# A Fourier mixing kernel with an ELU layer: one channel's transform, its loads and a batch's later transforms set to later steps

## The chip, the cores and the metric

The kernel runs on one core of a Trainium2 chip. Its time is the device time of one execution in microseconds (us); the figure used is the median over several executions. One further execution is recorded by the hardware profiler, and all rows of a profile in this text come from such an execution.

## The reference

```python
# x: (8, 3008, 256), w_in: (256, 2048), w_out: (2048, 256), all float32
X = np.fft.fft(x, axis=1)
X = np.fft.fft(X, axis=2)
attn = X.real.astype(np.float32)              # (8, 3008, 256)
h = attn.reshape(24064, 256) @ w_in
g = np.where(h > 0.0, h, np.exp(np.minimum(h, 0.0)) - 1.0)
out = (g @ w_out).astype(np.float32)
```

Each of the 8 batches is transformed along its 3008 rows and its 256 channels; only the real part is kept. Every row then goes through two matrix products with an ELU between them.

## The kernel before

**What is computed where.** The real part of the double transform is even in a joint mirroring of row and channel, so the kernel keeps two rings in SBUF, `Rr` (real) and `Ir` (imaginary), with the folded channels in their 128 partitions and half of the rows (1504 per batch, `HALF`) as columns. The channel transform is folded into the first weights (`Wc`, `Ws`). The channels are counted by 0 to 127 in the partitions; channel 128 is left over and is handled for all 8 batches together, in its own small transform. Its result is put into a third ring, `Rb`, which holds one row repeated in all partitions, and into partition 127 of `Ir`.

**Steps.** The columns of all batches are cut in 47 tiles of 256, and each tile in 8 steps (two blocks of 128 of the 2048 hidden units each): 376 steps in all. In a step TensorE forms `P` = Wc x Rr (`mm_P`), VectorE adds the part of channel 128 (`even_part`, tile `E`, line 764), TensorE adds `Q` = Ws x Ir onto the same PSUM bank `H`, and VectorE forms the mirrored half (`h_minus`, line 774). ScalarE makes the exponentials of both halves (line 394), VectorE the ELU (`g_plus`, `g_minus`, line 790, tile `G`). GpSimd forms four sums of blocks of `G` (`sum_1` to `sum_4`, line 391), and TensorE uses blocks and sums in seven products with `w2` and `WT` (`mm_X1`, `mm_X2`, PSUM banks `pA` to `pD`, line 382): a product scheme that needs seven multiplications for eight. Step n's second products are issued two steps later. After a tile's 8 steps the four banks are combined on ScalarE and VectorE (`comb_copy` with tile `p`, `comb_1`, `comb_2`, `comb_22`, `comb_3` with tiles `u` and `v`, line 388), transposed (`turn_u`, `turn_v`, lines 935 and 956, tile `ot`) and stored by SyncE (`store`, line 988, many small DMAs).

**Transforms.** A batch is loaded in four tiles `xl0` to `xl3` (`load_x`: `xl3` and `xl0` by SyncE, lines 168 and 169; `xl2` and `xl1` by indirect DMAs of GpSimd, line 157). GpSimd folds them in 16 operations of two pieces each (`fold_x`, line 476, tiles `e` and `o`); the results EO0, EO2, EO1 and EO3 feed four transforms (`at_dft`), real and imaginary part for even and odd rows. Each transform is done in two halves of three matrix products with the constant tiles `MC`, one at the end of a step and one at the end of the step two later. ScalarE copies the first half to a buffer `bs` (two buffers), and VectorE adds and subtracts both into the ring (`plus`, `minus`).

**Channel 128.** `load_ext` loads it in 16 pieces: four rows (j = 0 to 3) of 768 samples for 8 batches, four pieces each, sample by sample (line 613). When a row is there, it is stored to DRAM (`xe_dr`, line 631). `get_ext` loads all back in another layout (`xs`, line 637); `fold_ext` folds on GpSimd (`xe`); `dft_ext` is 12 products of 8 columns each, 24 instructions of TensorE; `ext_side` copies three parts to `bs` buffers on ScalarE; `ext_rows` combines them to `rx`, once on VectorE and once on GpSimd, and stores to DRAM (`r128`, lines 705 and 708); `spread_ext` loads a batch's part into `Rb` and `Ir` (lines 715 and 719).

**The order.** All is written as a list of events with due times in units of a step, `T = PERIOD`, and the list is sorted and issued. The due time sets only the place in the order of each engine; each engine then runs its instructions in that order as soon as what they wait for is there.

```python
    def at(t, fn):
        events.append((t, len(events), fn))
...
    for _, _, fn in sorted(events, key=lambda e: e[:2]):
        fn()
```

Computing instructions, the single-channel loads and `load_x`'s indirect loads of batch 1 are held in that order (`pin`); the other DMAs, among them `get_ext`, the output stores, the loads of `xl3` and `xl0` and `spread_ext`, are placed on SyncE's queue by the framework, which may put them elsewhere between the pinned ones. SyncE's queue issues in order and uses eight semaphores in turn, so that it waits for an earlier DMA's end before it issues the eighth after it.

Of the kernel before, what the change touches and what calls it, by code (L numbers as in the profile page):

```python
# [90 lines left out]
def kernel(  # L91
# [58 lines left out]
    def load_x(b):  # L150
        L = [
            spool.tile([128, 6 * ND], FP, tag=f"xl{j}", bufs=1, name=f"xl{j}")
            for j in range(4)
        ]
        for j in (2, 1):
            c = 1 if j == 2 else 2 if b == NB - 1 else 0
            load = nc.gpsimd.indirect_dma_start(
                out=L[j],
                out_offset=None,
                in_=xflat,  # L160
                in_offset=bass.IndirectOffsetOnAxis(
                    ap=ix[:, c : c + 1].bitcast(U32), axis=0
                ),
                element_offset=b * SEQ * ND,
            )
            if b == 1:
                pin(load)
        nc.sync.dma_start(out=L[3], in_=xrows(b, HALF, 6, 128))
        nc.sync.dma_start(out=L[0], in_=xrows(b, 0, 6, 128))
        if b == NB - 1:  # L170
            nc.gpsimd.dma_start(
                out=L[1][0:1, 0 : 5 * ND], in_=xrows(b, SEQ - 5, 1, 1, 5)
            )
        return L
# [218 lines left out]
    def act(o, i, func=AF.Copy, **kw):  # L393
        pin(nc.scalar.activation(out=o, in_=i, func=func, **kw))  # L394
# [211 lines left out]
    def load_ext(j, s0, s1):  # L606
        if j == 0 and s0 == 0:
            state["x1"] = spool.tile([128, HALF + 1], FP, tag="rx", bufs=1, name="x1")
        t = state["x1"][j * NB : (j + 1) * NB]

        def copy(s0, s1, row, step):
            pin(
                nc.sync.dma_start(
                    out=t[:, s0:s1],
                    in_=bass.AP(
                        tensor=xt,
                        offset=x.offset + row * ND + 128,
                        ap=[[SEQ * ND, NB], [step * ND, s1 - s0], [1, 1]],
                    ),
                )  # L620
            )

        with nc.allow_non_contiguous_dma(reason="one channel"):
            if j == 1 and s0 == 0:
                copy(0, 1, 0, 1)
                copy(1, s1, SEQ - 1, -1)
            else:
                step = -1 if j in (1, 2) else 1
                copy(s0, s1, (0, SEQ, HALF, HALF)[j] + step * s0, step)
        if s1 == 768:  # L630
            nc.sync.dma_start(out=xe_dr[j], in_=t[:, 0:768])
# [50 lines left out]
    def ext_side(g, rows=NB):  # L682
        n = NO if g > 1 else NE
        t = spool.tile([128, NE], FP, tag="bs", bufs=2, name="bs")
        act(t[0:rows, 0:n], state["ext"][32 * g : 32 * g + rows, 0:n])
        state["side", g] = t[0:rows, 0:n]

    def ext_rows(kodd, tt, rows=NB):
        n = NO if kodd else NE
        if not kodd or rows < NB:  # L690
            rx = spool.tile([128, HALF + 1], FP, tag="rx", bufs=1, name="rx")
            state["rx"] = rx[0:rows]
        if not kodd:
            a = state["ext"][0:NB, 0:n]
        else:
            a = state["side", 2]
        rx, b = state["rx"], state["side", 2 * kodd + 1]
        o, base = 1 - kodd, kodd * RUN
        m = n - 2 * o
        tt(rx[:, base : base + n], a, b, ALU.add)  # L700
        top = base + RUN - 1
        tt(rx[:, top : top - m : -1], a[:, o : o + m], b[:, o : o + m], ALU.subtract)
        if not kodd:
            tt(rx[:, HALF:], a[:, 0:1], b[:, 0:1], ALU.subtract)
            nc.sync.dma_start(
                out=r4_dr.rearrange("o b -> b o"), in_=rx[:, HALF : HALF + 1]
            )
        nc.sync.dma_start(
            out=r128_dr[0:rows, base : base + RUN], in_=rx[:, base : base + RUN]
        )  # L710

    def spread_ext(b, kodd):
        for sl, a, z in ring_cut(b * HALF + kodd * RUN, RUN, False):
            a, z = a + kodd * RUN, z + kodd * RUN
            nc.sync.dma_start(
                out=Rb[:, sl],
                in_=r128_dr[b : b + 1, a:z].to_broadcast([128, z - a]),
            )
            nc.sync.dma_start(out=Ir[127:128, sl], in_=r128_dr[b : b + 1, a:z])
# [359 lines left out]
    def at(t, fn):  # L1079
        events.append((t, len(events), fn))  # L1080
# [51 lines left out]
    T = PERIOD  # L1132
    for chunk, k in (
# [16 lines left out]
        first = (  # L1150
            (0.96, 0.96, 0.97, 1.9),
            (2.1, 2.9, 2.91, 4.22),
            (2.95, 2.96, 2.97, 4.2),
            (0.95, 0.96, 0.97, 4.2),
        )
# [98 lines left out]
    def safe(col):  # L1254

        return 8 * ((col - 1 - RING) // TW) + 8 if col > RING else 0
# [16 lines left out]
    def at_dft(step, gap, b, ri, kodd, stat):  # L1273
        box = []

        def d():
            if not box:
                box.append(Dft(ri, b, kodd, stat()))
            return box[0]

        at_half(step, d, 1, 0)
        at_half(step + gap, d, 0, b * HALF + (kodd + 1) * RUN)

    def begin_folds(b):
        state["EO"], state["ops"] = fold_x(state["L"], lambda key: nc.gpsimd, 2)
# [20 lines left out]
    for n in range(16):  # L1306
        j, k = divmod(n, 4)
        at(
            (14.4 + 0.25 * n) * T,
            lambda j=j, k=k: load_ext(j, 192 * k, 192 * (k + 1)),  # L1310
        )
    at(25.0 * T, get_ext)
    at(26 * T + 1.35, fold_ext)
    at(26 * T + 4.75, dft_ext)
    at(27 * T + 1.46, lambda: ext_side(1))
    at(27 * T + 1.47, lambda: ext_side(2))
    at(28 * T + 0.99, lambda: ext_rows(0, vtt))
    at(28 * T + 1.46, lambda: ext_side(3))
    at(29 * T + 1.35, lambda: ext_rows(1, gtt))
    fold_keys = [(k, p) for k in FOLDS for p in range(2 if k[0] not in "cx" else 1)]  # L1320
    n_big = sum(k[0] not in "cx" for k, _ in fold_keys)
    for b in range(1, NB):
        s0 = (b - 1) * steps_b
        l0 = s0 - 8 if b > 1 else 3.2
        at(l0 * T + 0.1, lambda b=b: state.update(L=load_x(b)))
        first = (6, 7, 7, 8, 9, 9, 10, 10, 12, 15)

        def fold_slot(n):
            if b > 1:
                return s0 - 1 + 39 * n // n_big  # L1330
            return first[n] if n < len(first) else 17 + int(0.92 * (n - len(first)))

        at(fold_slot(0) * T, lambda b=b: begin_folds(b))
        n = 0
        for key in fold_keys:
            slot = fold_slot(n)
            at(
                slot * T + (3.5 if slot < 16 else 1.3),
                lambda key=key: state["ops"][key](),
            )  # L1340
            n += key[0][0] not in "cx"
        for n, (ri, kodd) in enumerate(((0, 0), (1, 0), (0, 1), (1, 1))):
            at_dft(
                s0 + (28, 34, 38, 42)[n], 2, b, ri, kodd,
                lambda k=2 * ri + kodd: state["EO"][k],
            )
        for kodd in range(2):
            step = s0 + (28, 38)[kodd]
            assert step >= safe(b * HALF + (kodd + 1) * RUN)
            at(step * T + 1.0, lambda b=b, kodd=kodd: spread_ext(b, kodd))  # L1350
    last = total - 40
# [49 lines left out]
```

## Time and profile before

| | |
|---|---|
| median of 14 runs | 1982.52 us (1976.6 to 1986.67) |
| profiled execution | 1980.1 us |
| its span, first to last instruction | 1978.3 us |
| TensorE, busy | 1957.2 us (99%) |
| VectorE, busy | 1277.1 us (65%) |
| ScalarE, busy | 869.2 us (44%) |
| GpSimd, busy | 1361.1 us (69%) |
| mean granted TensorE clock | 0.998 |
| moved by DMA | 71.01 MB in 255546 packets, 243934 of them under 512 B |

PE is TensorE's products, PEld its weight loads, DVE VectorE, ACT ScalarE, POOL GpSimd and SP SyncE; SPq rows are DMAs that SyncE issues. L followed by a number is a line of the kernel before the change. A row of the timeline gives start, busy time, engine, line, operation, output and inputs, how many instructions were merged, and in brackets how long the engine had been idle and what ended that. The granted clock tells what share of its full rate TensorE was given.

### The profile page before, as it was taken

What the parts mean: (1) busy time and instruction counts of PE and PEld (TensorE: products, weight loads), DVE (VectorE), ACT (ScalarE), POOL (GpSimd) and SP (SyncE); (2) the same over time, 40 slices, a digit from 0 to 9 for tenths busy, and PEclk for the clock granted to TensorE, in tenths of its full rate; (3) what the DMA queues carried; (4) which work ended last, traced back from release to release, by engine and by line L of the source; (5) the groups of instructions that cost most, each with busy time, mean ns of one, the idle gap of its engine ahead of it and who ended that gap; (6) DMA issues with size and microseconds to landing.
All of it is one profiled execution on the core that took longest, in us unless ns stands there. A gap on an engine that the chain in (4) does not pass through costs nothing.

```text
span 1978.3 us, 26862 instructions
## 1 busy us (share of the span) xinstructions
PE 1957.2 (99%) x8912; PEld 1655.6 (84%) x8912; DVE 1277.1 (65%) x2325; ACT 869.2 (44%) x1668; POOL 1361.1 (69%) x1800
## 2 busy tenths in 40 slices
PE   9998999999999999999999999999999999999998
PEld 5786888888888888888888888888888888888887
DVE  8864656666566666666566665666556765566666
ACT  4653434444444434444444443444444444344443
POOL 3886748776587856787567875678657776455665
PEclk9999999999999999999999999999999999999999
DMA  8155110121011110011100211003010110100101
GB/s 332 54 22 89 34 16 19 31 61 22 14 19 43 45 29 11 18 45 45 26 17 14 63 27 26 12 19 88 8 21 11 20 22 14 16 12 12 22 10 24
DMA packets 255546, 71.01 MB, mean 36 GB/s; under 512 B 243934, under 2 KB 244850, under 8 KB 255024
## 3 DMA queue, kind: packets, MB, share of 16 engines
q1 hardware_dynamic: 250896, 56.46, 14.6%
q0 software_dynamic: 2336, 12.59, 2.0%
q8 instruction: 70, 1.15, 0.2%
q14 instruction: 68, 0.56, 0.1%
q10 hardware_dynamic: 2176, 0.26, 0.1%
HBM read 44.43 MB, written 24.80 MB: 35 GB/s over the span
## 4 chain that ended last, share of the span: by engine, by line
PE 95%; POOL 2%; DVE 1%; DMA 1%; ACT 1%; issue 0%; SPq 0%; POOLq 0%; DVEq 0%; ACTq 0%
PE H L382 38%; PE pC L382 16%; PE pD L382 16%; PE pB L382 16%; PE pA L382 8%; PE M L382 1%; POOL WT L391 1%; DMA xl<-in_x_dram 0%; DMA out_dram<-ot 0%; POOL G L391 0%; DVE E L764 0%; POOL w L391 0%; SPq L988 0%; DVE v L388 0%; ACT G L394 0%
## 5 line engine op out<-in xcount | busy, mean ns | idle before, releaser
L391 POOL TENSOR_TENSOR G<-G 128x256 f32<-128x256 f32 x1440 | 1034.6, 728 | 547.1 <-DVE G L790 438.1
L764 DVE SCALAR_TENSOR_TENSOR E<-Rb,wex,H 128x256 f32<-128x256 f32 x752 | 328.1, 478 | 613.0 <-PE H L382 609.7
L394 ACT ACTIVATE G<-H 128x512 f32<-128x512 f32 x376 | 224.5, 597 | 949.1 <-DVE G L774 943.8
L382 PE MATMUL H<-Ir,Ws 128*128 128x256 f32 x1504 | 387.4, 380 | 1.6 <-DVE E L764 1.6
L382 PE MATMUL H<-Rr,Wc 128*128 128x256 f32 x1504 | 387.0, 380 | 0.0
L382 PE MATMUL pC<-G,WT 128*128 128x256 f32 x1440 | 369.5, 379 | 0.0
L382 PEld LDWEIGHTS H<-Rr,Wc 128*128 128x128 f32 x1504 | 284.5, 190 | 56.4 <-issue 3.7
L382 PEld LDWEIGHTS H<-Ir,Ws 128*128 128x128 f32 x1504 | 277.1, 189 | 51.3 <-DVE E L764 5.0
L382 PEld LDWEIGHTS pC<-G,WT 128*128 128x128 f32 x1440 | 273.6, 190 | 37.2
L774 DVE SCALAR_TENSOR_TENSOR G<-E,H 128x512 f32<-128x512 f32 x376 | 257.3, 684 | 39.0 <-PE H L382 2.3
L790 DVE SCALAR_TENSOR_TENSOR G<-G,H 128x512 f32<-128x512 f32 x376 | 255.9, 681 | 28.6 <-ACT G L394 28.5
L790 DVE SCALAR_TENSOR_TENSOR G<-M,G 128x512 f32<-128x512 f32 x376 | 257.1, 684 | 0.0
L394 ACT ACTIVATE G<-G 128x512 f32<-128x512 f32 x376 | 233.3, 620 | 0.0
L382 PE MATMUL pA<-G,w 128*128 128x256 f32 x784 | 229.4, 379 | 0.7 <-DVE G L790 0.7
L382 PE MATMUL pB<-G,w 128*128 128x256 f32 x784 | 229.3, 379 | 0.0
L382 PE MATMUL pD<-G,w 128*128 128x256 f32 x784 | 229.3, 379 | 0.0
L394 ACT ACTIVATE M<-G 128x512 f32<-128x512 f32 x376 | 224.2, 596 | 0.0
L394 ACT ACTIVATE M<-M 128x512 f32<-128x512 f32 x376 | 221.0, 588 | 0.0
L382 PE MATMUL pB<-G,WT 128*128 128x256 f32 x720 | 214.7, 380 | 1.7 <-POOL G L391 1.7
L382 PE MATMUL pD<-G,WT 128*128 128x256 f32 x720 | 214.4, 379 | 1.6 <-DVE v L388 1.6
L382 PEld LDWEIGHTS pA<-G,w 128*128 128x128 f32 x784 | 148.9, 190 | 21.3 <-DVE G L790 1.1
L382 PEld LDWEIGHTS pD<-G,w 128*128 128x128 f32 x784 | 149.0, 190 | 20.3
(140 smaller groups left out, 1406.0 us busy)
## 6 DMA issues: line engine op xcount, KB each, us to landing
out_dram<-ot SPq DMA_DIRECT2D x496, 32.0 KB
xl<-in_x_dram SPq DMA_DIRECT2D x16, 768.0 KB
out_dram<-ot SPq DMA_DIRECT2D x256, 2.0 KB
Rb<-r SPq DMA_DIRECT2D x10, 376.0 KB
raw<-in_moe_w_in_dram SPq DMA_DIRECT2D x7, 512.0 KB
MC<-dft_mats SPq DMA_DIRECT2D x3, 1131.0 KB
raw<-in_moe_w_out_dram SPq DMA_DIRECT2D x4, 512.0 KB
out_dram<-ot SPq DMA_DIRECT2D x64, 28.0 KB
```

Source lines behind the costliest of these rows:

```text
L382: nc.tensor.matmul(out_, lhsT=lhsT, rhs=rhs, start=start, stop=stop, skip_group_check=True)
L391: pin(nc.gpsimd.tensor_tensor(out=o, in0=a, in1=b, op=op))
L394: pin(nc.scalar.activation(out=o, in_=i, func=func, **kw))
L764: nc.vector.scalar_tensor_tensor(out=S.E[:, c], in0=Rb[:, cols(i)], scalar=wex[:, f : f + 1], in1=S.H[:, c], op0=ALU.mult, op1=ALU.add,)
L774: nc.vector.scalar_tensor_tensor(out=two(S.G[:, 0:512])[:, :, ::-1], in0=two(S.E), scalar=2.0, in1=two(S.H), op0=ALU.mult, op1=ALU.subtract,)
L790: nc.vector.scalar_tensor_tensor(out=o, in0=e, scalar=-1.0, in1=h, op0=ALU.add, op1=ALU.max)
```

## The change

The loads of channel 128 are set half a step apart instead of a quarter, and `get_ext`, `fold_ext`, `dft_ext`, `ext_side` and `ext_rows` six steps later. In batch 1, the second, third and fourth transforms go two steps later each, the folds from the eleventh piece on come one step apart instead of 0.92, and the two calls of `spread_ext` move from steps 28 and 38 to 35 and 40. Nothing else is changed, and no instruction is added or removed.

```diff
     for n in range(16):
         j, k = divmod(n, 4)
         at(
-            (14.4 + 0.25 * n) * T,
+            (14.4 + 0.5 * n) * T,
             lambda j=j, k=k: load_ext(j, 192 * k, 192 * (k + 1)),
         )
-    at(25.0 * T, get_ext)
-    at(26 * T + 1.35, fold_ext)
-    at(26 * T + 4.75, dft_ext)
-    at(27 * T + 1.46, lambda: ext_side(1))
-    at(27 * T + 1.47, lambda: ext_side(2))
-    at(28 * T + 0.99, lambda: ext_rows(0, vtt))
-    at(28 * T + 1.46, lambda: ext_side(3))
-    at(29 * T + 1.35, lambda: ext_rows(1, gtt))
+    at(31.0 * T, get_ext)
+    at(32 * T + 1.35, fold_ext)
+    at(32 * T + 4.75, dft_ext)
+    at(33 * T + 1.46, lambda: ext_side(1))
+    at(33 * T + 1.47, lambda: ext_side(2))
+    at(34 * T + 0.99, lambda: ext_rows(0, vtt))
+    at(34 * T + 1.46, lambda: ext_side(3))
+    at(35 * T + 1.35, lambda: ext_rows(1, gtt))
...
     for b in range(1, NB):
         s0 = (b - 1) * steps_b
+        late = 2 if b == 1 else 0
...
-            return first[n] if n < len(first) else 17 + int(0.92 * (n - len(first)))
+            return first[n] if n < len(first) else 17 + n - len(first)
...
             at_dft(
-                s0 + (28, 34, 38, 42)[n], 2, b, ri, kodd,
+                s0 + (28, 34 + late, 38 + late, 42 + late)[n], 2, b, ri, kodd,
                 lambda k=2 * ri + kodd: state["EO"][k],
             )
         for kodd in range(2):
-            step = s0 + (28, 38)[kodd]
+            step = s0 + (35 if late else 28, 38 + late)[kodd]
             assert step >= safe(b * HALF + (kodd + 1) * RUN)
             at(step * T + 1.0, lambda b=b, kodd=kodd: spread_ext(b, kodd))
```

## The prediction

> **What bounds the kernel now.** I read the busy shares first, then the waits of TensorE, then the stretch around the longest one in the timeline and in the windows. TensorE is busy for 99% of the span, so only its holes can be won.
>
> ```profile
> PE 1957.2 (99%) x8912; PEld 1655.6 (84%) x8912; DVE 1277.1 (65%) x2325; ACT 869.2 (44%) x1668; POOL 1361.1 (69%) x1800
> ...
> PE H L382 <- POOL xe L391: 7.8, 1, 7.8
> PE pB L382 <- POOL G L391: 1.7, 2, 1.0
> ...
> PE pA L382 <- DVE G L790: 0.7, 1, 0.7
> ```
>
> The wait lines give total, times and longest. One wait is larger than all others together: TensorE stands 7.8 us before the transform of channel 128 (dft_ext), whose input `xe` GpSimd makes. In the timeline GpSimd itself waited there for a DMA:
>
> ```profile
> 177.37 0.28 SPq L631 DMA_DIRECT2D xe_dr<-x  x1
> 177.69 6.51 SPq L988 DMA_DIRECT2D out_dram<-ot  x13
> 184.25 0.45 SPq L637 DMA_DIRECT2D xs<-xe_dr  x1
> ...
> 186.53 0.38 POOL L391 TENSOR_TENSOR xs<-xs 128x96 f32<-128x96 f32 x1 [9.08 <-DMA xs<-xe_dr]
> ...
> 187.33 3.87 PE L382 MATMUL H<-MC,xe 128*8 128x377 f32 x24 [7.78 <-POOL xe L391]
> 191.13 1.13 PE L382 MATMUL H<-Rr,Wc 128*128 128x256 f32 x4
> ```
>
> The fourth row of channel 128 was written to DRAM at 177.37; its way back (`xs`) was issued on the same SyncE queue 6.9 us later, behind 13 output stores. TensorE had ended its work of step 26 at 179.55. The clock fell meanwhile (columns: span, then busy time and count by engine, then PEclk, DMA share, GB/s):
>
> ```profile
> 182.00:184.00 2.00, 0.00 (x0) 0.00 (x0) 0.00 (x0) 0.00 (x0) 0.00 (x0) 0.98 0.43 67
> 184.00:186.00 2.00, 0.00 (x0) 0.00 (x0) 0.00 (x0) 0.00 (x0) 0.00 (x0) 0.50 0.56 55
> 188.00:190.00 2.00, 2.00 (x18) 0.92 (x14) 0.00 (x0) 0.00 (x0) 1.84 (x4) 0.50 1.00 390
> ```
>
> Two smaller holes lie near, 1.04 us at 137.23 and together 1.32 us at 208.41 and 210.24. The two rows below lead to them.
>
> ```profile
> 134.07 1.97 POOL L476 TENSOR_TENSOR e<-e,e 128x384 f32<-128x384 f32 x2
> ...
> 206.73 0.49 ACT L394 ACTIVATE bs<-H 128x377 f32<-128x377 f32 x1 [3.70 <-POOL rx L391]
> ```
>
> **The change part by part.** No instruction is added or removed: all is moved. An undisturbed step takes 4.75 us (174.64 is the start of step 26; 155.6, 160.4, 165.1, 169.9 those of steps 22 to 25), half a batch transform adds 1.90 (200.74 to 202.64).
>
> *dft_ext six steps later.* It removes the wait of 7.78 if its input is ready. From 174.64: seven steps and two transform halves at the ends of 28 and 30 give 174.64 + 7 x 4.75 + 2 x 1.90 = 211.7 for the end of step 32, where it now stands. GpSimd's folding of `xs` comes about 2 us after the start of step 32 (206.9), so the input has to land by about 209.
>
> *Its loads half a step apart.* Each of the four rows is four loads of single elements, then a store to DRAM and a load back. In the trace four such loads in a row took 12.3 us (112.32 to the store at 124.80), 15.0 (125.12 to 140.14) and 12.3 (140.48 to 152.80). The built order of SyncE's queue is now: row 0 as before; row 1 between the stores of tiles 0 and 1; three loads of row 2, eight stores, the fourth load; then the load of batch 2's `xl3`, which waits for GpSimd's second `o3` fold, now in step 24; then the four loads of row 3; then batch 2's `xl0`; then row 3's store and load back, and only after these the 48 stores of tile 2. A fold's second piece starts about 0.9 us after a step's start and takes 1.18, so `xl3` goes out at 165.14 + 2.1 = 167.2. Add 15.0 for row 3 (the slowest of the three), 6.5 for the two `xl` (issued at 184.81 and landed by 191.4 in the trace; in full, since `xs` issued at 132.47 landed only at 139.85, after the loads ahead of it), and twice 2.3 for the store and load back (184.25 to 186.53): 193. With an indirect `xl` load beside it (172.26 to 179.56 in the trace) I allow up to 4 us, 197. That leaves 12 to 16 us, so I cost the loads at nothing. If the cover is gone, each us past 209 is a us of TensorE. The stores of tile 2 are pushed back to 193, and 48 at some 0.47 us (11.73 for 24) end at 216. The row of step 34 that goes out behind them (`r128`, then `Rb`) is due before step 40, past 245, so this costs nothing either.
>
> [...]
>
> *The clock.* The 24 instructions of dft_ext took 3.80 us (187.33 to 191.13) at clock 0.50, and four of them run side by side on 8 columns each. At full clock that is 1.90. A gain of 1.90 follows.
>
> The Trainium skill (TensorE: Matmul & The Clock Gate, section Terms) prices throttled time times (1 - K/N); the records here show 6.83 us at 0.5, which would make 3.4. But TensorE stood for the first half of that, already counted in the 7.78, so I take the row; the rule would add 1.5.
>
> *The folds one step apart.* Before, two pieces fell into step 17 (the 1.97 above) and GpSimd's first sums started at 135.99; TensorE waited 1.04 for them at 137.23. One piece of 0.97 moves to step 18: the sums start 0.97 earlier. Gain 1.0, bounds 0 and 1.04. The last fold is in step 38, its transform in 44; it hides under TensorE.
>
> *Batch 1's later transforms two steps later.* Each keeps the same instructions and the same gap of two steps. The second one, at the ends of 36 and 38, is added to the ring in step 39 and first read in step 40: VectorE's two additions (0.54 and 0.61 for the first transform) are done some 3 us into step 39, and TensorE reads them 7 us after its start. Cost nothing. Its copy now comes in step 37, so no transform's copy waits any more for the `bs` buffers that the rows of channel 128 hold: the 3.70 us of ScalarE at 206.73, and with it the 1.32 us of TensorE. Gain 1.32, bounds 0 and 1.32.
>
> *What comes instead at steps 33 to 35.* The side copies and the rows now meet the combining of tile 3. In step 33 ScalarE has `p` (0.38) and two side copies ahead of the exponentials, which delays them by 0.9 us; VectorE then enters step 34 some 0.7 late. In step 34 it has E 0.87, three rx 1.05, the pieces of u and v 0.41 and 0.68, and three of 0.68: 5.05 against 4.75. Beforehand (step 28, without combining) g_plus started 4.02 us after the step's start instead of 1.85, and a transform half at the end of the step hid that; now none stands there. Adding the 0.7 and the 0.60 of the combining, g_minus ends 6.6 after the start, and TensorE wants it at 5.6: a wait of 1.05. GpSimd's sums that need it take 0.75 and 0.8, so the one that TensorE reads is there at 8.2 against 7.5 (5.6 + 1.05 + 0.86): 0.7 more. In step 35 GpSimd has 3.03 of sums, 1.00 of fold and 1.91 of rx, 5.94 against 4.75, and with the lag I get 0.95. Sum 2.7, plus 0.15 where E delays the second matmuls of step 34: 2.85. Bounds: 0, if the slack holds more, and 5.0, if the sums repeat in step 36, where the half transform at its end covers.
>
> *Sum.* Gains 7.78 + 1.90 + 1.0 + 1.32 = 12.0; cost 2.85; net 9.15. The profiled execution took 1980.1 (span 1978.3 and 1.8 around it), 2.4 below the median of 1982.5. So 1970.9 against it, and 1973.3 against the median. A change under 0.2% (4 us) can't be told from none.
>
> **The rivals.** *Clean:* steps 33 to 35 hide all; gain 11 to 12.5, time 1970 to 1971.5. For it speaks that plain steps of the batches after show combining and transforms together with hardly a wait; against it, that VectorE's sum is over the step. *Dear seam:* the waits repeat in steps 36 to 39 or a transform's copy again stands behind a `bs` buffer; gain 4 to 7.5, time 1975 to 1978.5. *The change doesn't do what it says:* the wait only moves with the transform, as `xs` is again late by 8 us; then it lands at 217 instead of 193 to 197; time within 4 us of before. *Slower:* SyncE's queue. Behind the wait for the `o3` fold stand row 3, its store, its load back and 48 output stores; if row 3's single elements share the DMA engines badly with three loads of 768 KB, `xs` lands late and TensorE stands in step 32. It is worse than before by 4 us from a landing at about 222 (209 + 9.15 + 4): time 1987 and up, a us more for each us. Against it: 25 us over my sum, and in the trace the slowest row needed 16 us (161.40 to 177.37), stores between its loads.
>
> **How the numbers follow.** Forecast 0.60 (1971.5 to 1975), clean 0.13, dear seam 0.13, not effective 0.06, slower 0.08. The first three are faster by over 0.2%: 0.86; same 0.06; slower 0.08. The range 1969.5 to 1979.0 holds those three.
>
> **What would show it.** Right: no wait of TensorE for `xe`; no stretch at clock 0.50 before the tail; 24 instructions of dft_ext in 1.9 us near 211; `xs` landed by 197; waits of 1 to 4 us in all for DVE G and POOL G in steps 34 to 36; the wait at 137 gone. Wrong: a DMA wait ahead of `xs` in step 32, or waits for `Ir` or `Rb` at step 40.

## The result and the profile after

| | before | after |
|---|---|---|
| median | 1980.64 us (47 runs, 1976.08 to 1987.2) | 1970.84 us (10 runs, 1970.26 to 1971.07) |
| profiled span | 1978.3 us | 1968.8 us |
| ratio after to before, 95% interval | | 0.9946 [0.9935, 0.9958] |

The change makes the kernel 0.54% faster, 10.7 us of 1980.64 by the ratio, with an interval of 8.3 to 12.9; the two medians lie 9.8 us apart. The second thing in the table is the spread: 11 us before, 0.8 us after.

The waits of TensorE in the profile after, all of them (total, times, longest):

```profile
PE pD L382 <- DVE v L388: 2.5, 4, 1.0
PE H L382 <- DVE E L764: 1.9, 3, 1.1
PE M L382 <- DVE zero L369: 1.1, 1, 1.1
PE pB L382 <- POOL G L391: 0.5, 2, 0.4
PE pC L382 <- DVE u L388: 0.3, 1, 0.3
```

The wait for `xe` is gone; new are 1.0 us for `v` and 0.3 us for `u`. The timeline after shows the data's way, first SyncE's queue, then GpSimd, then TensorE:

```profile
185.66 0.29 SPq L631 DMA_DIRECT2D xe_dr<-x  x1
189.13 0.37 SPq L637 DMA_DIRECT2D xs<-xe_dr  x1
...
208.41 0.39 POOL L391 TENSOR_TENSOR xs<-xs 128x96 f32<-128x96 f32 x1
...
210.33 2.09 PE L382 MATMUL H<-MC,xe 128*8 128x377 f32 x24
212.35 1.13 PE L382 MATMUL H<-Rr,Wc 128*128 128x256 f32 x4
```

`xs` is issued at 189.13, five us later than before, and folded at 208.41 with no wait in brackets. dft_ext takes 2.02 us (210.33 to 212.35) instead of 3.80, and the windows give the clock there:

```profile
210.00:212.00 2.00, 2.00 (x26) 0.56 (x24) 0.00 (x0) 0.58 (x2) 1.84 (x4) 1.00 0.36 56
```

What is lost instead stands in steps 34 and 36. TensorE's timeline after, and behind it VectorE's rows of step 34:

```profile
219.99 1.13 PE L382 MATMUL H<-Ir,Ws 128*128 128x256 f32 x4 [0.31 <-DVE E L764]
221.38 1.10 PE L382 MATMUL pC<-G,WT 128*128 128x256 f32 x4 [0.26 <-DVE u L388]
223.46 0.67 PE L382 MATMUL pD<-G,WT 128*128 128x256 f32 x2 [0.98 <-DVE v L388]
...
231.41 0.70 PE L382 MATMUL pB<-G,WT 128*128 128x256 f32 x2 [0.38 <-POOL G L391]
```

```profile
219.85 1.05 DVE L388 TENSOR_TENSOR rx<-H,bs 8x377 f32<-8x377 f32 x3
220.83 0.40 DVE L388 TENSOR_TENSOR u<-v,pC 128x256 f32<-128x256 f32 x1
222.03 0.69 DVE L790 SCALAR_TENSOR_TENSOR G<-G,H 128x512 f32<-128x512 f32 x1 [0.80 <-ACT G L394]
222.63 0.68 DVE L388 TENSOR_TENSOR v<-v,pD 128x512 f32<-128x512 f32 x1
```

The rows of channel 128 (`rx`) stand ahead of the `u` that TensorE's `pC` waits for, and VectorE's wait for ScalarE ahead of the `v` that `pD` waits for.

From the starts of each step's first product in the timelines I take the steps' lengths. These are the steps in which the profiled executions differ by over 0.3 us (4.75 is a plain step, 6.65 one with half a transform at its end):

| step | before | after | read as |
|---|---|---|---|
| 18 | 6.06 | 5.09 | the fold piece's wait, 0.97 gained |
| 26 | 16.50 | 4.75 | wait and dft_ext gone from here: 11.75 |
| 30 | 8.51 | 6.65 | 1.86 gained |
| 32 | 4.75 | 6.86 | dft_ext now here: 2.11 |
| 34 | 6.65 | 7.20 | before with half a transform, after without: 2.45 lost |
| 36 | 6.65 | 7.29 | 0.64 lost |
| 46 | 4.75 | 6.65 | the half transform that left step 34, nothing lost |

0.97 + 11.75 - 2.11 + 1.86 - 2.45 - 0.64 = 9.38, against 9.58 us between the two spans (1978.33 and 1968.75). The start, which the change does not touch, differs by 0.49 more, and later steps take 0.29 back, step 261 most of it (4.95 before, 5.17 after).

### The profile page after: what moved, and what is told of

It reads as the page before. It is cut to its first block, busy times and chain, and to the rows that moved or that the text cites. A ratio compares the mean times of both kernels' runs of the same rounds, so it can differ in the third digit from the quotient of the medians.

```text
span 1968.8 us, 26858 instructions
## 1 busy us (share of the span) xinstructions
PE 1955.6 (99%) x8912; PEld 1654.3 (84%) x8912; DVE 1277.3 (65%) x2325; ACT 869.1 (44%) x1668; POOL 1361.2 (69%) x1800
## 4 chain that ended last, share of the span: by engine, by line
PE 95%; DVE 2%; POOL 1%; ACT 1%; issue 0%; DMA 0%; DVEq 0%
PE H L382 38%; PE pC L382 16%; PE pD L382 16%; PE pB L382 16%; PE pA L382 8%; PE M L382 1%; POOL WT L391 1%; DVE E L764 0%; POOL G L391 0%; POOL w L391 0%; DVE v L388 0%; DMA Rb<-r 0%; DVE pow L281 0%; DVE G L774 0%; DVE u L388 0%
## 5 line engine op out<-in xcount | busy, mean ns | idle before, releaser
L382 PEld LDWEIGHTS pB<-G,w 128*128 128x128 f32 x784 | 148.9, 190 | 20.4 <-PE H L382 0.2
```

Of the source, the lines that this page charges most:

```text
L382: nc.tensor.matmul(out_, lhsT=lhsT, rhs=rhs, start=start, stop=stop, skip_group_check=True)
```

## The experiments

Two theories were put against each other. The first is the prediction's sum: one long wait for data and its half clock, two small waits, and a new seam where the rows of channel 128 meet the combining of tile 3. The rival gave the whole gain to one part and nothing to the others, or laid a wait to something else; each run has its own. Every kernel was measured beside the kernel before, whose median was 1980.64 us in the result's series and 1984.37 to 1985.3 in those of the experiments; ratios are to the before of the same series, while comparisons with the changed kernel's 1970.84 go across series.

**Channel 128 alone** (ext_alone). The changed kernel with

```diff
-        late = 2 if b == 1 else 0
+        late = 0
...
-            return first[n] if n < len(first) else 17 + n - len(first)
+            return first[n] if n < len(first) else 17 + int(0.92 * (n - len(first)))
...
-            step = s0 + (35 if late else 28, 38 + late)[kodd]
+            step = s0 + (35 if b == 1 else 28, 38)[kodd]
```

> Only channel 128 is moved: its loads half a step apart, everything from get_ext to ext_rows six steps later, and batch 1's first spread_ext to step 35 with it. The folds stay 0.92 of a step apart and batch 1's transforms stay at 34, 38 and 42. Theory 1 (the sum of the prediction): the hole of 7.8 us and the half clock's 1.9 us go, the fold's hole of 1.0 us near 137 stays, and the second transform's copy, now in step 35, stands behind the bs buffers that the rows of channel 128 hold: 1 to 2 us lost there. Gain over the kernel before 7 to 8.7 us. Rival: the moved folds and transforms are worth nothing, all of the change's gain is in channel 128: gain 9.3 to 9.8 us.

1971.6 us (1971.42 to 1972.15), span 1969.8, 1.0 over the changed kernel's; ratio to before 0.9939 [0.9921, 0.9956]. The gain was 8.5 us by the spans, inside theory 1's 7 to 8.7, but 12.8 by the medians, above both expectations, which were reckoned from the one profiled execution of before. Steps 18 (6.08), 34 (9.10, with half a transform of 1.90 now at its end) and 36 (7.31) hold the difference: the 1.0 of the fold is missing, as theory 1 said, and the seam is the same 2.45 and 0.66 as in the changed kernel. Of the loss at `bs` it said 1 to 2 us, and that was a miss. ScalarE did stand there, but TensorE did not pay: the half transform at the end of step 34 covers it. The row of ScalarE's timeline in this kernel:

```profile
230.48 0.49 ACT L394 ACTIVATE bs<-H 127x377 f32<-127x377 f32 x1 [3.55 <-POOL rx L391]
```

So moving batch 1's later transforms is worth nothing that this comparison shows; the folds one step apart were worth 1.0 us, and channel 128 the rest.

**The rest alone** (rest_alone). The kernel before with the folds one step apart, `34 + late, 38 + late, 42 + late` and the second spread_ext at `38 + late`.

> Only the folds (one step apart) and batch 1's second to fourth transform (two steps later, its second spread_ext at step 40) are moved; channel 128 stays as before. Theory 1: the hole of 1.0 us near 137 closes, but the arrival of xs is set by SyncE's queue and not by TensorE, so TensorE comes 1.0 us earlier to the same arrival and waits 8.8 us instead of 7.8: gain 0 to 0.4 us in all. Rival: the parts add up, and the 1.0 us shows in the total: gain 0.9 to 1.5 us.

1982.88 us (1978.7 to 1989.32) against 1984.37; ratio 0.9999 [0.9986, 1.0012]. The interval holds both expectations. In the profile step 18 fell to 5.12 and the wait for `xe` was 7.8 again, but its `xs` was issued at 181.87 instead of 184.25, and such arrivals differ from run to run by more than the us in question. In that execution GpSimd also issued an indirect load of 1.01 us (at 184.76) between the folding of `xs` and the making of `xe`, which it did not before. Whether a us won ahead of that wait is swallowed by it stays open.

**The load earlier on the queue** (early_xs). The kernel before with

```diff
-    at(25.0 * T, get_ext)
+    at(18.2 * T, get_ext)
```

> The kernel before, with one due time changed: get_ext at 18.2 instead of 25.0 steps, so that the last load of xs stands on SyncE's queue behind three output stores after xe_dr instead of thirteen. dft_ext stays at step 26. Theory 1: the wait was for that load's place on the queue; it is issued when xe_dr has landed, near 180.4, and lands near 182.6; TensorE's wait falls from 7.8 to 3 to 4.5 us, and with it part or all of the stretch at half clock: gain 3.5 to 6 us. Rival: dft_ext waits for GpSimd's turn or for the single-channel loads themselves: wait 7 to 8 us as before, gain under 0.5 us.

1979.07 us (1972.0 to 1983.39); ratio 0.9973 [0.9957, 0.9989], 5.3 us with an interval of 2.2 to 8.5. SyncE's queue in its timeline:

```profile
178.85 0.28 SPq L631 DMA_DIRECT2D xe_dr<-x  x1
179.18 2.03 SPq L988 DMA_DIRECT2D out_dram<-ot  x3
181.57 0.38 SPq L637 DMA_DIRECT2D xs<-xe_dr  x1
```

From store to load back are 2.7 us instead of 6.9, and TensorE's wait was 5.3 instead of 7.8 in an execution whose `xe_dr` came 1.5 us later (by that alone 9.3). So the place on the queue held some 4 us of the wait, an estimate from one execution each; the wait left is still above the 3 to 4.5 expected, and the half clock stayed: dft_ext took 4.11 us (184.64 to 188.75) at a clock of 0.50 up to 188.7. What is left of the wait lies in the single-element loads, the store and the load back, which no run here takes apart.

**The half step alone** (half_only). The kernel before with

```diff
-            (14.4 + 0.25 * n) * T,
+            (14.4 + 0.5 * n) * T,
```

> The kernel before with only the loads of channel 128 set half a step apart; its transform stays at step 26. Theory 1 (the half step makes the data later, and only the six steps hide it): the last xs is issued near 189 as in the changed kernel and lands near 191.5, so TensorE waits 12 to 15 us before dft_ext instead of 7.8, with dft_ext at half clock: 4 to 8 us slower than before. Rival (spreading the loads frees the queue and brings the data earlier): wait under 7.8, not slower.

In the profile the wait was as expected:

```profile
PE H L382 <- POOL xe L391: 13.3, 1, 13.3
```

`xs` went out at 189.34, against 189.13 in the changed kernel. But the time, 1985.76 us (1983.04 to 1987.32) against 1985.3, ratio 1.0005 [0.9994, 1.0016], was not 4 to 8 us slower: a miss. The expectation was reckoned from the one profiled execution of before, of 1980.1 us. Against its span, 1978.3 us, this kernel's 1984.2 is 5.9 longer, as expected; but the before of this series has a median 5.2 us above that execution. That its `xs` usually comes later than 184.25 fits this, and is not shown.

**The quarter step with the six steps** (quarter). The changed kernel with the line above turned back.

> The changed kernel with the loads of channel 128 a quarter of a step apart again, as before; all else as changed. Theory 1 (any arrival by 207 is hidden, the half step gives nothing): xs is issued near 184, no wait before dft_ext, time within 0.6 us of the changed kernel's 1970.8. Rival (the half step keeps the queue free for the output stores, which free VectorE's and SyncE's buffers): 1 us or more slower than the changed kernel.

1970.71 us (1970.31 to 1971.61), the changed kernel's 1970.84 within their spreads: the half step is worth nothing here. There is no wait for `xe`, though in its profile `xs` was issued not near 184, as expected, but at 194.02, ten us after that of before in the same order of the queue:

```profile
184.22 0.28 SPq L631 DMA_DIRECT2D xe_dr<-x  x1
184.54 8.46 SPq L988 DMA_DIRECT2D out_dram<-ot  x13
194.02 0.38 SPq L637 DMA_DIRECT2D xs<-xe_dr  x1
```

With dft_ext at step 26 each us of such lateness would be one of TensorE's; six steps later all of it is covered. This fits the times: the five kernels with dft_ext at step 32 spread over 0.7 to 1.4 us, those with it at step 26 over 4.3 to 13 us (bs_three, run once, aside). In the runs of before of quarter's series the mean granted clock was 0.997 to 0.998 in those under 1982 us and 0.995 to 0.996 in those over 1984, so the longer ones also had more of the half clock.

**The clock by itself** (warm, warm_long). The kernel before with, in dft_ext (50 in warm_long),

```diff
         ps = state["ext"] = bank("H")
+        for _ in range(32):
+            mm(ps, zero, zero[:, 0:1].to_broadcast([128, 512]), True)
         for t in range(3):
```

> The kernel before with 32 products of zeros (512 columns each, some 6.9 us) put ahead of dft_ext's own products into the same PSUM bank, which those then overwrite; nothing else is changed, and TensorE still waits for xe. Theory 1 (half the cost of the clock is apart from the wait): the clock stays at 1.00 through the hole, dft_ext takes 1.9 to 2.1 us instead of 3.8, and the profiled span is 1.5 to 2.2 us shorter than that of a run with the same arrival of xs. Rival (24 instructions of 8 columns are bound by something else than the clock): still 3.5 us or more, span unchanged.

In the profile the expectation was missed: `xs` came late (187.34), 3.74 us of the wait stayed uncovered, and dft_ext took 3.60 (190.51 to 194.11) with the clock falling 0.8 us after its start. So this execution says nothing of the clock's price. The time was 1981.45 us (1976.9 to 1987.4), ratio 0.998 [0.9964, 0.9995], 4.0 us with an interval of 1.0 to 7.1. The longer one:

> As the kernel warm, with 50 products of zeros (some 10.8 us) ahead of dft_ext instead of 32, so that TensorE is busy up to the arrival of xe or nearly; dft_ext's own products are unchanged. Theory 1 (dft_ext took 3.8 us because of the clock alone): the clock stays at 1.00 from the start to the tail, dft_ext takes 2.0 to 2.2 us, and 1.6 to 2 us are gained against a run with the same arrival of xs; the wait for xs itself is not shortened, so that most of the change's gain is missing: profiled span 1975 to 1983. Rival: dft_ext still takes over 3 us.

TensorE's timeline, and behind it the window that holds most of dft_ext:

```profile
179.60 10.83 PE L382 MATMUL H<-zero 128*128 128x512 bf16 x49
192.40 2.32 PE L382 MATMUL H<-MC,xe 128*8 128x377 f32 x24 [1.97 <-POOL xe L391]
194.64 1.13 PE L382 MATMUL H<-Rr,Wc 128*128 128x256 f32 x4
```

```profile
192.00:194.00 2.00, 1.60 (x22) 0.91 (x24) 0.00 (x0) 0.00 (x0) 1.91 (x4) 1.00 0.96 378
```

The clock stays at 1.00 and dft_ext takes 2.24 us (192.40 to 194.64) instead of 3.80, a little over the 2.2 expected, though TensorE still waits 1.97 us for `xe`. So 1.56 us are the clock's, apart from the wait. The time, 1981.62 us (1980.79 to 1988.41), ratio 0.9989 [0.9973, 1.0006], can't show 1.6 us beside the spread of the arrival.

**A third buffer** (bs_three). The kernel before with `bufs=3` instead of 2 at both places where a `bs` tile is made.

> The kernel before with three bs buffers instead of two; nothing else is changed. Theory 1 (the 1.9 us that TensorE loses in step 30 come from the first transform's copy standing behind bs buffers that the rows of channel 128 hold): ScalarE's wait of 3.7 us for rx goes and step 30, 8.51 us, falls to 6.65 to 7.2. Rival (GpSimd's rows and VectorE's delay make the loss by themselves): step 30 stays over 8 us.

One execution, 1978.27 us: step 30 fell from 8.51 to 6.65 (207.47 to 214.12), and the copy no longer waits:

```profile
202.98 0.48 ACT L394 ACTIVATE bs<-H 128x377 f32<-128x377 f32 x1
```

Its span is 1976.5, 1.8 under before's with the same wait for `xe` (7.82). So those 1.86 us were the `bs` buffers, whole. In the changed kernel the first transform comes before channel 128, and these 1.86 us go without a third buffer.

**The rows one step later** (rows_later). The changed kernel with

```diff
-    at(34 * T + 0.99, lambda: ext_rows(0, vtt))
-    at(34 * T + 1.46, lambda: ext_side(3))
-    at(35 * T + 1.35, lambda: ext_rows(1, gtt))
+    at(35 * T + 0.99, lambda: ext_rows(0, vtt))
+    at(35 * T + 1.46, lambda: ext_side(3))
+    at(36 * T + 1.35, lambda: ext_rows(1, gtt))
...
-            step = s0 + (35 if late else 28, 38 + late)[kodd]
+            step = s0 + (36 if late else 28, 38 + late)[kodd]
```

> The changed kernel with ext_rows, the third side copy and batch 1's first spread_ext one step later (rows on VectorE in step 35, on GpSimd in step 36, spread in step 36), so that VectorE's rows no longer share step 34 with the combining of tile 3. Theory 1 (VectorE is over its step in step 34 and TensorE pays): step 34, 7.2 us in the changed kernel, falls to 4.75 to 5.4, and step 35 stays under 5.2; gain over the changed kernel 1.3 to 2.6 us, 10.8 to 12 over the kernel before. Rival: the same waits only come a step later: within 0.5 us of the changed kernel.

1969.14 us (1968.51 to 1969.31), ratio to before 0.9925 [0.9908, 0.9943]; span 1966.9, 1.9 under the changed kernel's and 11.4 under before's, by the spans both as expected. Step 34 is 5.47, a little over the 5.4 expected, step 35 is 4.75. Of the four waits two are left:

```profile
219.84 1.13 PE L382 MATMUL H<-Ir,Ws 128*128 128x256 f32 x4 [0.31 <-DVE E L764]
229.61 0.70 PE L382 MATMUL pB<-G,WT 128*128 128x256 f32 x2 [0.43 <-POOL G L391]
```

**The copies behind the exponentials** (sides_later). rows_later with

```diff
-    at(33 * T + 1.46, lambda: ext_side(1))
-    at(33 * T + 1.47, lambda: ext_side(2))
+    at(33 * T + 4.9, lambda: ext_side(1))
+    at(33 * T + 4.91, lambda: ext_side(2))
...
-    at(35 * T + 1.46, lambda: ext_side(3))
+    at(35 * T + 4.9, lambda: ext_side(3))
```

> The kernel of rows_later with the side copies on ScalarE set behind the step's exponentials instead of ahead of them: the first two at 33 T + 4.9, the third at 35 T + 4.9 (it is read in step 36). Theory 1 (what is left of the seam, 0.7 us in step 34 and 0.7 in step 36, is ScalarE's copies delaying the exponentials and so VectorE and GpSimd): step 34 falls from 5.47 to 4.75 to 4.95 and step 36 from 7.35 to 6.65 to 6.9; 0.8 to 1.4 us faster than rows_later. Rival (it is VectorE's and GpSimd's rows themselves): within 0.3 us of rows_later.

1967.73 us (1967.04 to 1968.41), ratio to before 0.9917 [0.9902, 0.9931]; span 1965.3. Steps 34 and 36 are 4.75 and 6.65, plain ones: nothing of the seam is left. The waits of TensorE in this kernel, all of them:

```profile
PE H L382 <- DVE E L764: 1.6, 2, 1.1
PE pD L382 <- DVE v L388: 1.6, 3, 0.5
PE M L382 <- DVE zero L369: 1.1, 1, 1.1
```

ScalarE and VectorE around step 34 to 35 show how: the two copies come after the step's exponentials, and g_plus follows the three rx at once, where in rows_later it waited 1.06 us for ScalarE, and in the changed kernel 0.80.

```profile
217.68 0.96 ACT L394 ACTIVATE bs<-H 8x377 f32<-8x377 f32 x2
...
223.57 1.05 DVE L388 TENSOR_TENSOR rx<-H,bs 8x377 f32<-8x377 f32 x3
224.55 0.67 DVE L790 SCALAR_TENSOR_TENSOR G<-G,H 128x512 f32<-128x512 f32 x1
```

This version beats both kernels: its runs lie wholly under those of the changed kernel, 3.1 us between the medians, and 3.0 under quarter, which was measured in the same series.

## Why the prediction was right

The forecast was faster, 1973.3 us and 1969.5 to 1979.0; 1970.84 was measured. That lies in the range, but not in the forecast's own band (1971.5 to 1975): it is in that of the rival *clean* (1970 to 1971.5). The profile decides between them: the seam that *clean* denies cost 3.09 us, and the forecast came out 2.5 us high because 2.4 had been added that don't belong there (below).

*The long wait and its clock.* 7.78 and 1.90 were 9.68; steps 26 and 32 give 11.75 - 2.11 = 9.64. warm_long shows the clock's share apart. It was 1.78 in the changed kernel (3.80 to 2.02) against 1.90: the prediction halved all of the 3.80, but before, the clock was back at 1.00 for the last 0.37 of it (0.81 in the window 190 to 192). The product of throttled time and share that the Trainium skill gives (TensorE: Matmul & The Clock Gate, section Terms) would have made 3.4 of it; TensorE stood for half of those 6.83 us, so the row served better here.

*The loads hidden.* `xs` was expected to land by 193 to 197; it was issued at 189.13 and landed at 192.96, by the record of its semaphore in the trace. The quarter run shows that the half step was not needed, and that the 12 to 16 us of slack were not idle caution: issued at 194.02 in one execution, the load was still covered. One row was misread, without effect: the first row's loads took 12.5 us (112.32 to 124.80), not 12.3.

*The folds.* 1.0 expected, 0.97 in step 18; ext_alone, which leaves the folds as before, has step 18 at 6.08 again.

*The `bs` buffers.* Right mechanism, wrong size: 1.32 were the two idle gaps, but step 30 lost 1.86. In a plain step each group of products starts some 0.16 us before the end that the trace gives for the one before, and the group after a gap took 0.70 instead of 0.59; a gap costs both on top, twice 0.27. bs_three gives 1.86 back. Wrong was only to name batch 1's later transforms for it: the first transform's copy is the one that stood there, and it is freed because channel 128 now comes after it.

*The seam.* 2.85 expected, 2.45 + 0.64 = 3.09 measured. The overfull VectorE of step 34 was right, and rows_later confirms it; sides_later shows that ScalarE's copies ahead of the exponentials made the rest. The place where TensorE pays was wrong. The prediction had it wait in step 35 for g_minus and a sum. It waits within step 34, because that is the first step in which the next tile writes its sums to `pC` and `pD`: it can't begin there before VectorE's late comb_22 and comb_3 have read the old tile's (the 0.26 and 0.98 for `u` and `v`). Step 35 then was a plain one (4.75); the 0.95 reckoned for GpSimd's full step came out as 0.64, in step 36.

*Against the median.* This step failed. 1980.1 - 9.15 = 1970.95 was the sum against the profiled execution, and 1970.84 was measured; I then added 2.4 because that execution lay below the median. But the executions differ in just the wait that the change removes: before the change they spread over 11 us, after it over 0.8. And the traces of before, early_xs and half_only, which differ in the loads of channel 128 alone, agree to 0.6 us in every step but 26 (16.50, 14.27 and 22.17 us). What a stall makes vary goes with the stall, so nothing was to be added. That the sum came within 0.11 us of the median (0.43 of the profiled 1970.52) is partly luck: `bs` was 0.54 too small and the seam 0.24, which partly cancel, and the untouched start differed by 0.49.

Of the rivals, *slower* was far: the load had some 15 us in hand (192.96 against the fold at 208.41). *Clean* was not this kernel, but sides_later shows that it was there to be had.

## What to carry to other kernels

Where the bounding engine has one long wait for data, moving the consumer to a later place in its order can take the wait away if its result has slack, and here took the half clock and the run-to-run spread along with it; making the data earlier (early_xs) won only a part. Then look at what the moved work now stands beside: here three copies and three small additions, set a fraction of a step otherwise, were worth another 3 us. And when the term removed is the one that varies, reckon against the time of the execution in which it was read.

## What the runs showed of the hardware that was not expected

In these traces the clock fell and rose on a fixed grid. The stretches of constant clock in the records of these kernels, but for the last one of each, last 3.41 us (warm), 6.83 (before, early_xs, rest_alone, bs_three) and 13.65 (half_only) at 0.5, and 177.49, 184.32, 1781.76 (bs_three) and 1785.17 at 1.0: one, two and four, and 52, 54, 522 and 523 times 3.413 us. In warm the clock fell after TensorE was at work again: it stood from 186.77 to 190.51 and its clock dropped at 191.3, as its windows show.

```profile
188.00:190.00 2.00, 0.00 (x0) 0.00 (x0) 0.00 (x0) 0.00 (x0) 0.29 (x1) 1.00 0.78 101
190.00:192.00 2.00, 1.49 (x14) 0.78 (x18) 0.00 (x0) 0.00 (x0) 1.92 (x5) 0.83 0.98 381
192.00:194.00 2.00, 2.00 (x14) 0.45 (x6) 0.00 (x0) 0.00 (x0) 1.84 (x4) 0.50 0.81 331
```

The Trainium skill, TensorE: Matmul & The Clock Gate, section What's actually happening, gives a free-running window of 3413 ns, with which these stretches agree. A wait of 3.74 us was already enough to halve the clock in warm, one of 1.97 us in warm_long was not; and covering 6.9 us of a hole of 10.7 saved only 0.2 us of dft_ext's time in warm's profile (3.60 against 3.80 us).

The other thing is how much the same queue of single-element loads varies: with the same order of SyncE's queue, the last `xs` was issued at 181.87 (rest_alone), 184.18 (bs_three), 184.25 (before), 187.34 (warm), 189.19 (warm_long) and 194.02 (quarter). Why it varies so much was not tried.
